# K turned in its own order, joint softmax sums, and weight transfers from GpSimd in a fused attention and maxout kernel

## The chip, the cores and the metric

The kernel runs on one core of a Trainium2 chip. A core has five engines with queues of their own: TensorE (PE; its weight loads are listed apart as PEld), VectorE (DVE), ScalarE (ACT), GpSimd (POOL) and SyncE (SP). SP, ACT and POOL can start DMA transfers, which 16 DMA engines carry out. The metric is the device time of one execution in microseconds; lower is better.

## The reference

Block-causal attention over 8 batches, 8 heads, 576 positions of 64 dimensions in blocks of 64, and then a feed-forward layer that takes the largest of three products. q, k and v are f32, the weights double precision; the kernel computes in f32, and splits its operands into a high and a low part where one f32 product of reduced precision would not do.

```python
scores = (1 / sqrt(D)) * q @ k.T             # q, k, v: (8, 8, 576, 64)
scores = where(block_i >= block_j, scores, -1e9)
attn = softmax(scores)                       # denominators + 1e-9
x = (attn @ v).transpose(0, 2, 1, 3).reshape(4608, 512)
h = max(x @ w1, x @ w2, x @ w3)              # w: (512, 768)
out = h @ w_out                              # (768, 512)
```

## The kernel before

**The order of the work.** The program isn't written in the order in which it runs. `job(cost, rank, call, after=, take=, give=)` describes one step: which engines can do it and at what estimated cost, a rank (its due time, in units near a microsecond), the jobs it follows, and the buffers it takes and gives back (`slots` says how many there are). `in_order` then plays a greedy schedule over all jobs and writes the instructions in the order that comes out. The numbers at the head (`LAG`, `SEND`, `LOAD`, `DMA`, `MOVE`, `TURNED`, `GAP`, `SMALL`) and the functions `pe`, `dve`, `act`, `pool` are its prices: they take no time themselves, but they set the order of every engine's queue. On the chip each engine follows its queue strictly in order and waits at an instruction until its inputs are there.

**Attention.** Two heads make a `Pair`, 64 partitions each; four pairs make a batch. Batch 0 is done in two parts, `FRONT` (queries and keys below 256) and `BACK` (queries from 256, all keys); batch 1 is `EARLY`, the others `WHOLE`. The steps of a pair:

- `load`: q and k come in 32x32 blocks into the tiles `qn` and `kn` (four DMAs each), v into `vn`.
- `turn_k`, `turn_q`: VectorE turns the 32x32 blocks into `kq`. K is written scattered, so that in each block of 128 a run of 32 places holds the keys of one remainder modulo four; Q is written in order.
- `qk`: scores on PE, one f32 matmul per head and query tile (the trace lists two records for each); `ask` and `qk4` do the last 64 queries of both heads in one stationary operand, `q8`.
- `top` (line 405): VectorE finds the negative row maximum; `exp` (485): ScalarE's exponential with row sums; `sum` and `inverse` (490, 493): small VectorE instructions on the sums, for each head apart; `scale` (414 on ScalarE or 416 on POOL): normalises.
- `turn` (510, 514): VectorE turns P into the tile `pz`; `move` (520): four DMAs send each head's `pz` to `pt`, the P^T that PE reads.
- `pv` (754): P^T against V gives x, `out` copies it, `x_high` and `x_low` split it into `xh` and `xl`.

**Weights.** 24 units, 18 of w1, w2, w3 and 6 of w_out. Each `Unit` loads 512 KB of doubles (line 277), and takes them apart into an f32 high part and a low part: |w| on ScalarE (287), five VectorE steps (293, 300, 306, 312, 323), a copy on ScalarE, three matmuls on PE (330 to 332), a last copy on ScalarE. `DELAY` and `PACE` set the ranks of the units, `NEAR` how many units ahead a load may be issued.

**The layer.** A `Chunk` is half a batch, 256 or 320 columns of x. `product` (867) multiplies three pairs of parts (w high with xh and xl, w low with xh) over four slices of x for each of 6 x 3 weight units, `most` takes the maxima (882), `high` and `low` split h into `hh` and `hl`, and `project` (933) multiplies by w_out. The products fill PE between the attention steps.

Of the kernel before, what the change touches and what calls it, by code (L numbers as in the profile page):

```python
# [19 lines left out]
INF = 3.0e38  # L20
# [14 lines left out]
SEND = 650.0  # L35
LOAD = 475.0
DMA = 2000.0
MOVE = 3500.0
TURNED = 3000.0

GAP = 125.0
SMALL = 75.0
# [82 lines left out]
def pe(*cols, least=128):  # L125
    return sum(max(n, least) / 2.4 + 2.7 for n in cols)


def dve(n, fast=False):
    return 70.0 + n / (1.92 if fast else 0.96)  # L130


def act(n, psum=True):
    return (52.0 if psum else 95.0) + n / 1.2


def pool(n):
    return 190.0 + 1.95 * n
# [3 lines left out]
def kernel(  # L142
# [23 lines left out]
    DELAY = 16.0  # L166
    PACE = 4.0
# [7 lines left out]
    NEAR = 2  # L175
    XB = 1
# [43 lines left out]
    nats = {nm: const.tile([P, S], F32, name=nm) for nm in ("qn", "kn")}  # L220
# [21 lines left out]
    class Unit:  # L242


        def __init__(self, u, src, dst, n, prior, *early):
# [8 lines left out]
                {"SP": LOAD},  # L254
                rank - 4,
# [19 lines left out]
        def load(self, eng):  # L275
            st = moe.tile([P, 1024], F32, name=self.tag, bufs=1).bitcast(I32)
            nc.sync.dma_start(st.rearrange("p (c f) -> p c f", f=2 * self.n), self.src.bitcast(I32))
            lo_hi = st.rearrange("p (n t) -> p n t", t=2)
            self.low_word, self.high_word = lo_hi[:, :, 0].bitcast(U32), lo_hi[:, :, 1]
# [68 lines left out]
    def weights():  # L348
# [8 lines left out]
        for f in range(NF):  # L357
# [7 lines left out]
                early[u - NEAR],  # L365
# [43 lines left out]
    def norm_cost(n):  # L409
        return {"POOL": 160.0 + 1.66 * n, "ACT": 188.0 + n / 1.2}  # L410
# [7 lines left out]
    class Head:  # L418
# [5 lines left out]
        def plan(self, t0, after):  # L424

            pair, part, scales, later = self.pair, self.pair.part, {}, []
            for n, ts in enumerate(part.groups):
                apart, exps, r = None, [], t0 + (SECOND if part.beside and ts == part.later else n)
                for t in ts:
                    m = P * (t + 1)  # L430
                    d = job(
                        {"DVE": dve(m)},
# [3 lines left out]
                        after=(pair.scored[ts], apart),  # L436
                        take=("stat",) if t == part.tiles[0] else (),
                    )
                    if t != ts[-1]:
                        apart = job({}, 0, lambda eng: None, after=(d,), lasts=GAP)  # L440
                    exps.append(job({"ACT": act(m) + 185.0}, r + 2, self.exp, t, after=(d,), take=(f"p{t}",)))
                join(exps, BANK)
                later += exps
                if ts in part.first and ts != part.first[-1]:
                    continue
                done = [t for ts in part.first for t in ts] if ts in part.first else ts
                cols = slice(min(COL[t] for t in done), max(COL[t] for t in done) + 1)
                inv = job({"DVE": SMALL}, r + 4, self.sum, cols, after=later, lasts=SMALL + GAP)
                inv = job({"DVE": SMALL}, r + 4, self.inverse, cols, after=(inv,))
                for t in done:  # L450
                    scales[t] = job(norm_cost(P * (t + 1)), r + 5 + t / 2, self.scale, t, after=(inv,))
                later = []
            join(scales.values(), ("stat",))
# [4 lines left out]
            for t in part.tiles:  # L458
# [6 lines left out]
                    take=() if first else ("pz",),  # L465
# [5 lines left out]
            self.moved = job(  # L471
                {"SP": 4 * SEND}, t0 + 13, self.move, after=self.turned, take=("pt",), give=("pz",), lasts=4 * SEND + TURNED
            )
            return first

        def top(self, eng, t):

            if not hasattr(self, "stat"):
                self.stat = tuple(att.tile([P, NT], F32, name=nm, bufs=slots["stat"]) for nm in ("nm", "sm", "rs"))
# [9 lines left out]
        def sum(self, eng, c):  # L489
# [537 lines left out]
```

## Time and profile before

| | us |
|---|---|
| median of 3 runs (lowest, highest) | 934.22 (932.08, 934.27) |
| the profiled execution | 933.72 |
| its span, first to last instruction | 931.9 |
| PE busy | 886.0 |
| PE's weight loads busy | 735.1 |
| DVE busy | 560.9 |
| ACT busy | 457.9 |
| POOL busy | 246.1 |

The page of a profile gives busy time of each engine, the span in 40 slices, the DMA queues, the chain of work that ended last, and the costliest groups of instructions by line, tile and shape. An engine in the list of waits stands before the arrow, what released it behind; "SPq" is SyncE's own queue of DMA issues. The views by window show the same for a stretch of time, and the timeline lists instructions with start, duration and, in brackets, the idle time before. Matmul records overlap one another, so what a matmul costs is read from start to start, not from its own duration.

### The profile page before, as it was taken

Reading aid. Unit: us, or ns where it says so; the run is one execution under the profiler, and the core shown is the slowest. Engines: PE = TensorE matmul, PEld = TensorE weight load, DVE = VectorE, ACT = ScalarE, POOL = GpSimd, SP = SyncE. Lnnn points to the kernel's source line nnn. Section 1 sums busy time; section 2 is a strip of 40 time slices with the busy share of each in tenths; the row PEclk is TensorE's granted clock in tenths of the full one; section 3 lists DMA queues with packets and bytes.
Section 4 is the critical chain, followed back from the end, with each engine's and each line's share of the span. In section 5 each row is a group of like instructions: output and inputs, shape, how many; then the busy total and the mean of one; then the engine's idle time right before and its main releaser. Section 6 shows DMA issues by size and latency. Waiting matters only on the chain.

```text
span 931.9 us, 17031 instructions
## 1 busy us (share of the span) xinstructions
PE 886.0 (95%) x5736; PEld 735.1 (79%) x5736; DVE 560.9 (60%) x1768; ACT 457.9 (49%) x1315; POOL 246.1 (26%) x368
## 2 busy tenths in 40 slices
PE   3778988999999999999999999999999999999998
PEld 2346755877888978897888978897888978899997
DVE  5888999787764376547664386447664376431101
ACT  3655565676554365536554355536554355532111
POOL 2123212334231232213231232223231232222201
PEclk9889999999999999999999999999999999999999
DMA  5778567676653455552753355552763354330010
GB/s 119 178 186 229 147 165 158 141 154 151 145 128 73 94 132 115 127 109 53 161 125 74 83 133 122 119 110 58 149 135 69 84 133 96 95 72 23 1 34 23
DMA packets 253910, 104.93 MB, mean 113 GB/s; under 512 B 206464, under 2 KB 248448, under 8 KB 253824
## 3 DMA queue, kind: packets, MB, share of 16 engines
q1 hardware_dynamic: 234624, 101.49, 47.3%
q10 hardware_dynamic: 19200, 2.36, 1.6%
q8 instruction: 45, 0.74, 0.3%
q14 instruction: 41, 0.34, 0.1%
HBM read 41.94 MB, written 9.44 MB: 55 GB/s over the span
## 4 chain that ended last, share of the span: by engine, by line
PE 77%; DVE 10%; DMA 6%; issue 2%; ACT 2%; SPq 1%; POOL 0%; DVEq 0%; ACTq 0%
PE pm L867 44%; PE pm L933 15%; PE sb L754 8%; PE sb L706 7%; PE sb L712 2%; DMA w<-in_moe_w_dram 2%; DVE pz L510 2%; DMA qn<-in_q_dram 2%; DVE sb L405 2%; ACT p L485 1%; DMA pt<-pz 1%; DMA kn<-in_k_dram 1%; DVE left L323 1%; SPq L520 1%; DVE kq L683 1%
## 5 line engine op out<-in xcount | busy, mean ns | idle before, releaser
L867 PE MATMUL pm<-xh,w 128*128 128x320 f32 (+1 forms) x2304 | 491.2, 302 | 2.5 <-ACT xh L234 1.6
L867 PEld LDWEIGHTS pm<-xh,w 128*128 128x128 f32 x2304 | 378.2, 190 | 18.1 <-issue 8.8
L867 PE MATMUL pm<-xl,w 128*128 128x256 f32 (+1 forms) x1152 | 341.9, 297 | 3.0 <-POOL xl L239 3.0
L867 PEld LDWEIGHTS pm<-xl,w 128*128 128x128 f32 x1152 | 219.5, 191 | 6.5 <-POOL xl L239 3.9
L405 DVE CUSTOM_DVE_ANT_0 sb<-sb,mask 128x384 f32<-128x384 f32 (+4 forms) x288 | 135.6, 505 | 89.5 <-PE sb L706 44.1
L882 DVE TENSOR_TENSOR m<-pm,m 128x256 f32<-128x256 f32 (+1 forms) x192 | 86.3, 449 | 165.2 <-PE pm L867 164.5
L510 DVE STREAM_TRANSPOSE pz<-p 128x384 f32<-128x384 f32 (+3 forms) x320 | 159.6, 528 | 37.6 <-ACT p L414 17.7
L485 ACT ACTIVATE p<-sb,nm 128x256 f32<-128x256 f32 (+3 forms) x256 | 134.3, 527 | 93.6 <-DVE nm L405 75.9
L416 POOL TENSOR_TENSOR p<-p,rs 128x128 f32<-128x128 f32 (+4 forms) x148 | 108.3, 751 | 244.1 <-DVE rs L493 168.7
L239 POOL TENSOR_TENSOR hl<-m,hh 128x256 fp32r<-128x256 f32 x96 | 71.4, 744 | 288.1 <-ACT hh L234 258.0
L933 PE MATMUL pm<-wo,hh 128*128 128x512 f32 x384 | 123.8, 403 | 0.4 <-ACT wo L234 0.4
L234 ACT CAST hh<-m 128x256 fp32r<-128x256 f32 x96 | 39.0, 406 | 157.6 <-DVE m L882 157.5
L754 PE MATMUL sb<-pt,vn 128*64 128x320 f32 (+4 forms) x896 | 103.3, 364 | 4.8 <-DMA pt<-pz 3.1
L706 PE MATMUL sb<-kq 64*128 64x384 f32 (+3 forms) x512 | 91.8, 478 | 16.7 <-DVE kq L690 16.7
L754 PEld LDWEIGHTS sb<-pt,vn 128*64 128x64 f32 x896 | 62.4, 138 | 45.7 <-issue 14.9
L414 ACT ACTIVATE p<-p,rs 128x256 f32<-128x256 f32 (+4 forms) x140 | 82.3, 603 | 24.1 <-DVE rs L493 17.7
L706 PEld LDWEIGHTS sb<-kq 64*128 64x128 f32 x512 | 47.1, 197 | 54.6 <-issue 21.3
L239 POOL TENSOR_TENSOR xl<-x,xh 128x320 fp32r<-128x320 f32 (+1 forms) x64 | 52.2, 819 | 142.9 <-ACT xh L234 142.9
L933 PEld LDWEIGHTS pm<-wo,hh 128*128 128x128 f32 x384 | 70.5, 188 | 18.2 <-issue 1.7
L933 PE MATMUL pm<-wo,hl 128*128 128x512 f32 x192 | 75.0, 391 | 0.0
L234 ACT COPY m<-pm 128x256 f32<-128x256 f32 (+1 forms) x96 | 38.1, 397 | 33.2 <-PE pm L867 21.7
L485 ACT ACTIVATION_READ_ACCUMULATOR p<-sb,nm 128x1 f32 x256 | 50.3, 196 | 0.0
(67 smaller groups left out, 691.7 us busy)
## 6 DMA issues: line engine op xcount, KB each, us to landing
pt<-pz SPq DMA_DIRECT2D x224, 200.0 KB, 3.9
w<-in_moe_w_dram SPq DMA_DIRECT2D x18, 512.0 KB, 4.8
kn<-in_k_dram SPq DMA_DIRECT2D x128, 72.0 KB, 2.4
vn<-in_v_dram SPq DMA_DIRECT2D x64, 128.0 KB, 2.5
out_dram<-osb SPq DMA_DIRECT2D x32, 256.0 KB, 2.0
qn<-in_q_dram SPq DMA_DIRECT2D x96, 72.0 KB, 2.4
pt<-pz SPq DMA_DIRECT2D x32, 152.0 KB, 3.2
wo<-in_moe_w_out_dram SPq DMA_DIRECT2D x6, 512.0 KB, 4.6
```

Source lines behind the costliest of these rows:

```text
L234: nc.scalar.copy(dst, src)
L239: {"DVE": nc.vector, "POOL": nc.gpsimd}[eng].tensor_tensor(out=dst, in0=a, in1=b, op=ALU.subtract)
L405: nc.vector.tensor_tensor_reduce(out=ps, in0=ps, in1=hidden, scale=-SCALE, scalar=first, op0=ALU.add, op1=ALU.min, accum_out=out_)
L414: nc.scalar.mul(p, p, r)
L416: nc.gpsimd.tensor_tensor(out=p, in0=p, in1=r.broadcast_to([P, p.shape[1]]), op=ALU.mult)
L485: nc.scalar.activation(self.p[t], self.ps.pop(t), AF.Exp, bias=nm[:, c : c + 1], scale=-1.0, accum_out=sm[:, c : c + 1])
L510: nc.vector.transpose(dst, p[:, 0 : n * P])
L706: nc.tensor.matmul(ps, self.q[h.own, P * t : P * (t + 1)], self.k[h.own, 0:w], start=True, stop=True)
L754: nc.tensor.matmul(o[h.own].rearrange("p (i u) -> p i u", u=n)[:, :, c0 : c0 + z - a], self.vn[:, kt, h.j, :], h.pt[:, :, a:z], start=(m = ...
L867: nc.tensor.matmul(self.ps, w[i, f][:, c, :], xx, start=(c == 0 and s == 0), stop=(c == NC - 1 and s == 2))
L882: nc.vector.tensor_tensor(out=m, in0=ps, in1=m, op=ALU.max)
L933: nc.tensor.matmul(self.po[: self.rows], h, w[f], start=(f == 0 and s == 0), stop=(f == NF - 1 and s == 2))
```

## The change

- **K in its own order.** q and k share one tile `nat` and one transpose turns both into `kq` in the order in which they lie (`turn_qk`, in place of `turn_k` and `turn_q`). The order that P^T needs is made when PE reads K: `keys` gives it an access pattern whose inner step is four elements. `qk4` takes its 576 keys as 256 and 256 + 64 instead of 288 + 288.
- **Joint sums.** The row statistics of two heads lie in one tile; `sum` and `inverse` move from Head to Pair and work on both heads once all exponentials are done.
- **One P^T for two heads in batch 0.** There both heads share `pz` and `pt`, the second at an offset of 96, and `move` is issued once.
- **GpSimd starts the weights' transfers**, with NEAR 4 instead of 2 (w_out's own limit stays 2).
- **Buffers:** P^T 2 instead of 3 (and `stat` counted by pair), x32 2 instead of 1 of each half.
- **The planner:** new prices, DELAY 28 and PACE 3.5 instead of 16 and 4; the second chunk's products from f = 2 on wait for the first chunk's projection.

```diff
-SEND = 650.0
-LOAD = 475.0
-DMA = 2000.0
-MOVE = 3500.0
-TURNED = 3000.0
+SEND = 620.0
+LOAD = 540.0
+ASK = 1000.0
+DMA = 2200.0
+MOVE = 4500.0
+TURNED = 4400.0
...
-    return sum(max(n, least) / 2.4 + 2.7 for n in cols)
+    return sum(max(n, least) / 2.4 + 13.5 for n in cols)
...
-    DELAY = 16.0
-    PACE = 4.0
+    DELAY = 28.0
+    PACE = 3.5
...
-    NEAR = 2
-    XB = 1
+    NEAR = 4
+    XB = 2
...
-        sb=5, sb5=4, scores=4, pm=3, stat=4, stat4=2, p0=2, p1=2, p2=2, p3=2, p4=1,
+        sb=5, sb5=4, scores=4, pm=3, stat=2, stat4=2, p0=2, p1=2, p2=2, p3=2, p4=1,
...
-        vn=2, kq=2, q8=2, pz=2, pt=3,
+        vn=2, kq=2, q8=2, pz=2, pt=2,
...
-    nats = {nm: const.tile([P, S], F32, name=nm) for nm in ("qn", "kn")}
+    nat = const.tile([P, 2, S], F32, name="nat")
...
-                {"SP": LOAD},
-                rank - 4,
+                {"POOL": ASK},
+                rank - 8,
                 self.load,
...
-            nc.sync.dma_start(st.rearrange("p (c f) -> p c f", f=2 * self.n), self.src.bitcast(I32))
+            nc.gpsimd.dma_start(st.rearrange("p (c f) -> p c f", f=2 * self.n), self.src.bitcast(I32))
...
+            self.off = 96 * j if pair.part.loads == 1 else 0
...
-            self.moved = job(
-                {"SP": 4 * SEND}, t0 + 13, self.move, after=self.turned, take=("pt",), give=("pz",), lasts=4 * SEND + TURNED
-            )
+            if alone or self.j:
+                turned = self.turned if alone else self.turned + pair.heads[0].turned
+                self.moved = job(
+                    {"SP": 4 * SEND}, t0 + 13, self.move, after=turned, take=("pt",), give=("pz",), lasts=4 * SEND + TURNED
+                )
+                if not alone:
+                    pair.heads[0].moved = self.moved
...
+                pair.stats = tuple(att.tile([P, 2, NT], F32, name=nm, bufs=slots["stat"]) for nm in ("nm", "sm", "rs"))
+            self.stat = tuple(t[:, self.j] for t in pair.stats)
...
-        def sum(self, eng, c):
-            nc.vector.tensor_scalar_add(self.stat[2][:, c], self.stat[1][:, c], EPS)
...
+            if self.off:
+                self.pair.heads[0].pt, run = self.pt, slice(0, 192)
...
+                    exps = [h.exps[t] for h in self.heads for t in ts]
+                    inv = job({"DVE": SMALL}, r, self.sum, cols, after=exps, lasts=SMALL + GAP)
+                    inv = job({"DVE": SMALL}, r, self.inverse, cols, after=(inv,))
...
+        def sum(self, eng, c):
+            _, sm, rs = self.stats
+            nc.vector.tensor_scalar_add(rs[:, :, c], sm[:, :, c], EPS)
...
-        def turn_k(self, eng):
-
+        def turn_qk(self, eng):
             kq = att.tile([P, 2, S], F32, name="kq", bufs=slots["kq"])
-            self.k, self.q = kq[:, 0], kq[:, 1]
-            src, dst, n = nats["kn"][:, self.at :], self.k, min(self.part.keys, 512)
-            nc.vector.transpose(dst[:, 0:n].rearrange("p (k j r) -> p k r j", j=4, r=32), src[:, 0:n])
-            if n == self.part.keys:
+            self.q, self.k = kq[:, 0], kq[:, 1]
+            own, n = self.part.queries, self.part.keys
+            if n < S:
+                nc.vector.transpose(kq[:, :, 0:n], nat[:, :, self.at : self.at + n])
                 return
-            nc.vector.transpose(dst[:, 512:S].rearrange("p (j r) -> p r j", j=4), src[:, 512:S])
-
-        def turn_q(self, eng):
-            own = self.part.queries
-            nc.vector.transpose(self.q[:, own], nats["qn"][:, self.at :][:, own])
+            src, dst = (t.rearrange("p a s -> p (a s)")[:, own.start :] for t in (nat, kq))
+            nc.vector.transpose(dst, src)
+
+        def keys(self, own, a, z):
+
+            n = min(P, z - a)
+            return self.k[own, a:z].rearrange("p (k r j) -> p k j r", j=4, r=n // 4)
...
-                        nc.tensor.matmul(ps, self.q[h.own, P * t : P * (t + 1)], self.k[h.own, 0:w], start=True, stop=True)
+                        nc.tensor.matmul(ps, self.q[h.own, P * t : P * (t + 1)], self.keys(h.own, 0, w), start=True, stop=True)
...
-            ps = self.ps[a] = psa.tile([P, 288], F32, name="sb")
-            nc.tensor.matmul(ps, self.q8, self.k[:, 288 * a : 288 * a + 288], start=True, stop=True)
+            ps = self.ps[a] = psa.tile([P, 256 + 64 * a], F32, name="sb")
+            nc.tensor.matmul(ps[:, 0:256], self.q8, self.keys(slice(0, P), 256 * a, 256 * a + 256), start=True, stop=True)
+            if a:
+                nc.tensor.matmul(ps[:, 256:], self.q8, self.keys(slice(0, P), 512, S), start=True, stop=True)
...
-                        h.pt[:, :, a:z],
+                        h.pt[:, :, h.off + a : h.off + z],
...
+            wait = prior.projected if prior and prior.first else None
+            self.first = not prior
...
-                            after=(last, xjobs[c], units[i, f].done),
+                            after=(last, xjobs[c], units[i, f].done, wait if f > 1 else None),
...
+            self.projected = prior
```

More of the change, by code (lines that the diff above doesn't have):

```diff
@@ L422, in __init__, with plan @@
             self.ps, self.p = {}, {}
-        def plan(self, t0, after):
-            pair, part, scales, later = self.pair, self.pair.part, {}, []
+            self.off = 96 * j if pair.part.loads == 1 else 0
+        def plan(self, t0):
+            pair, part, self.exps, self.inv = self.pair, self.pair.part, {}, {}
             for n, ts in enumerate(part.groups):
-                apart, exps, r = None, [], t0 + (SECOND if part.beside and ts == part.later else n)
+                apart, r = None, t0 + (SECOND if part.beside and ts == part.later else n)
                 for t in ts:
@@ L435, in plan, with turns @@
                         t,
-                        after=(pair.scored[ts], apart),
-                        take=("stat",) if t == part.tiles[0] else (),
+                        after=(pair.scored[ts], apart, pair.began),
+                        take=("stat",) if pair.began is None else (),
                     )
+                    pair.began = pair.began or d
                     if t != ts[-1]:
                         apart = job({}, 0, lambda eng: None, after=(d,), lasts=GAP)
[L441 to L453, printed above, removed]
+                    self.exps[t] = job({"ACT": act(m) + 240.0}, r + 2, self.exp, t, after=(d,), take=(f"p{t}",))
+                join([self.exps[t] for t in ts], BANK)
+        def turns(self, t0, after):
+            pair, part, self.scales = self.pair, self.pair.part, {}
+            for t in part.tiles:
+                r = t0 + 8 + t / 2 + (SECOND if part.beside and t in part.later else 0)
+                self.scales[t] = job(norm_cost(P * (t + 1)), r, self.scale, t, after=(self.inv[t],))
+            scales, alone = self.scales, part.loads == 2
             self.turned, first = [], None
@@ L464, in plan @@
                     after=(scales[t], first or after),
-                    take=() if first else ("pz",),
+                    take=() if first or (self.j and not alone) else ("pz",),
                 )
@@ L500, in turn @@
             if not hasattr(self, "pz"):
-                self.pz = att.tile([P, 4 * (RUN + 16)], F32, name="pz", bufs=slots["pz"])
+                if self.j and self.pair.part.loads == 1:
+                    self.pz = self.pair.heads[0].pz
+                else:
+                    self.pz = att.tile([P, 4 * (RUN + 16)], F32, name="pz", bufs=slots["pz"])
             z = self.pz.rearrange("p (j u) -> p j u", u=RUN + 16)
@@ L554, in plan @@
                 part.first,
-                after=(tk, tq, before and before.later),
+                after=(tq, before and before.later),
                 take=2 * len(part.first) * BANK,
@@ L595, in plan4 @@
             for a in range(2):
-                last = job({"PE": 4 * pe(288)}, first + 3 + a, self.qk4, a, after=(asked, last), take=BANK)
+                last = job({"PE": 4 * pe(256, *(64,) * a)}, first + 3 + a, self.qk4, a, after=(asked, last), take=BANK)
                 tops.append(
                     job(
-                        {"DVE": dve(288) + 10.0},
+                        {"DVE": dve(288) + 120.0},
                         first + 4 + a,
@@ L606, in plan4 @@
                 )
-            e = job({"ACT": 2 * act(288) + 370.0}, first + 5, self.exp4, after=tops, take=("p4",), give=2 * BANK)
+            e = job({"ACT": act(256) + act(320) + 480.0}, first + 5, self.exp4, after=tops, take=("p4",), give=2 * BANK)
             inv = job({"DVE": SMALL}, first + 6, self.sum4, after=(e,), lasts=SMALL + GAP)
@@ L641, in finish @@
                 )
-            join((prior,), ("pt", "pt", "vn"))
+            join((prior,), ("pt",) * self.part.loads + ("vn",))
         def values(self, eng):
```

67 lines of the change are left out of this document (45 added, 22 removed).

## The prediction

> **What bounds the kernel now.** I read the page first, then the stages, then who waits for whom in the stage that loses time. The page gives each engine's share and 40 slices of the span.
>
> ```profile
> PE 886.0 (95%) x5736; PEld 735.1 (79%) x5736; DVE 560.9 (60%) x1768; ACT 457.9 (49%) x1315; POOL 246.1 (26%) x368
> ...
> PE   3778988999999999999999999999999999999998
> ...
> DVE  5888999787764376547664386447664376431101
> ```
>
> TensorE (PE) is full from about the eleventh slice on, and VectorE (DVE) only in slices two to seven. So there are two stages; the busy times per window tell them apart.
>
> ```profile
> 0.00:50.00 50.00, 27.76 (x96) 13.85 (x96) 35.62 (x121) 25.54 (x73) 11.11 (x27) 0.93 0.65 151
> 50.00:100.00 50.00, 41.44 (x219) 28.86 (x221) 43.32 (x105) 26.22 (x58) 13.50 (x14) 0.90 0.80 217
> 100.00:150.00 50.00, 43.46 (x236) 28.59 (x233) 48.87 (x132) 32.26 (x82) 15.52 (x17) 1.00 0.65 156
> 150.00:200.00 50.00, 48.68 (x303) 38.51 (x301) 40.56 (x127) 29.21 (x88) 12.80 (x19) 1.00 0.62 131
> 200.00:250.00 50.00, 48.38 (x307) 38.86 (x307) 39.89 (x137) 32.05 (x101) 19.14 (x29) 1.00 0.68 151
> ...
> 500.00:550.00 50.00, 50.00 (x361) 42.58 (x361) 29.98 (x99) 24.79 (x73) 13.43 (x18) 1.00 0.40 85
> ```
>
> The columns are PE, weight loads, DVE, ScalarE (ACT), GpSimd (POOL), granted clock, DMA share and GB/s. At 500 us PE issues 361 matmuls in 50 us without a gap: nothing on another engine shortens that stage. In the first 150 us it issues 551, and DVE is busy 127.8 of 150 us: the ramp is VectorE's. It ends when VectorE hands over the last of the 24 weight units and PE has used it:
>
> ```profile
> 158.96 0.68 DVE L323 SCALAR_TENSOR_TENSOR left<-wo,osb 128x512 fp32r<-128x512 uint32 x1
> ```
> ```profile
> 161.91 0.39 PE L332 MATMUL pm<-left,plus 128*128 128x512 f32 x1
> ```
>
> Behind that PE loses little: 1.3 and 1.6 us of the next two windows. So the sum is: how much earlier does the last unit come, what has PE then left to do, and what does the change cost PE itself. The profiled execution took 933.72 us (span 931.9 and 1.8 around it), 0.5 below the median of 934.22. All sums are against 933.7.
>
> **VectorE's work ahead of the last unit.** The order is needed here. VectorE before, first pair of heads; L490 and L493 are the sum and its inverse, kq the turned K and Q:
>
> ```order
> L405 ISA nm 128x1
> L490 TENSOR_SCALAR rs<-sm 128x2
> L493 RECIPROCAL rs<-rs 128x2
> L490 TENSOR_SCALAR rs<-sm 128x2
> L493 RECIPROCAL rs<-rs 128x2
> L683 STREAM_TRANSPOSE kq<-kn 128x2x32x4
> L690 STREAM_TRANSPOSE kq<-qn 128x256
> ```
>
> VectorE after, the same place (L294 to L313 are steps of the first weight unit):
>
> ```order
> L294 TENSOR_SCALAR wo_134<-wo_134 128x512
> L301 TENSOR_SCALAR wo_134<-wo_134 128x512
> L722 STREAM_TRANSPOSE kq<-nat 128x2x256
> L625 TENSOR_SCALAR rs<-sm 128x2x2
> L307 SCALAR_TENSOR_TENSOR wo_134<-w_100,wo_134 128x512
> L629 RECIPROCAL rs<-rs 128x2x2
> L313 TENSOR_SCALAR wo_134<-wo_134 128x512
> ```
>
> One transpose where two or three stood, two small instructions where four stood, and weight steps between. Counted to the last unit, VectorE has 374 rows before and 331 after; all kinds agree but four: 18 turns of K and 11 of Q become 11 joint ones (4 front, 4 back, 3 whole pairs), 40 sums and inverses become 20, and of 14 maxima and 7 copies of x there stay 12 and 4. Their prices:
>
> ```profile
> L683 DVE STREAM_TRANSPOSE kq<-kn 128x512 f32<-128x512 f32 x32 | 35.4, 1107 | 6.4 <-PE sb L706 6.2
> ...
> L690 DVE STREAM_TRANSPOSE kq<-qn 128x576 f32<-128x576 f32 x28 | 21.2, 758 | 0.0
> ...
> L882 DVE TENSOR_TENSOR m<-pm,m 128x320 f32<-128x320 f32 x96 | 45.9, 479 | 51.5 <-PE pm L867 51.3
> ...
> L493 DVE RECIPROCAL rs<-rs 128x3 f32<-128x3 f32 x56 | 9.7, 173 | 1.2
> ...
> L686 DVE STREAM_TRANSPOSE kq<-kn 128x64 f32<-128x64 f32 x32 | 8.6, 269 | 0.0
> ...
> L490 DVE TENSOR_SCALAR rs<-sm 128x2 f32<-128x2 f32 x16 | 3.9, 241 | 2.7 <-ACT p L485 2.7
> L493 DVE RECIPROCAL rs<-rs 128x2 f32<-128x2 f32 x16 | 2.5, 157 | 0.1
> L683 DVE STREAM_TRANSPOSE kq<-kn 128x256 f32<-128x256 f32 x4 | 2.4, 604 | 5.3 <-DMA vn<-in_v_dram 4.5 <-DMA kn<-in_k_dram 0.8
> L690 DVE STREAM_TRANSPOSE kq<-qn 128x320 f32<-128x320 f32 x4 | 2.0, 498 | 0.0
> L236 DVE COPY x<-sb 128x320 f32<-128x320 f32 x4 | 1.9, 477 | 0.0
> ...
> L690 DVE STREAM_TRANSPOSE kq<-qn 128x256 f32<-128x256 f32 x4 | 1.6, 400 | 0.0
> ```
>
> The columns are busy us, mean ns, idle before. K costs more than Q per column because it is written scattered: from 256 to 512 columns 503 ns, 1.96 ns a column, while Q (256 to 576) takes 358 ns, 1.12 ns a column with 113 ns fixed. The joint turn writes in order, so I price it by Q: 0.69, 1.12 and 1.40 us for 512, 896 and 1152 columns. A front pair saves 604+400-686 = 318 ns, a back pair 1107+269+498-1116 = 758, a whole pair 1107+269+758-1403 = 731: 4, 4 and 3 of them, 6.5 us. Sums: 16 pairs of 241+157 and 4 pairs of about 173+173 are 7.7 us; 20 instructions of 173 remain, 3.5: 4.2 us saved. Two maxima (0.96) and three copies (1.4) stand later or on ScalarE. Together 13.1 us; neighbours on VectorE overlap by some tenth, so I take **12 us**. Ends: 0, if the joint sums, which now wait for both heads' exponentials, leave as much idle time as they save; 13.1.
>
> **Waits for weights.** Of VectorE's idle time before 160 us these rows belong to transfers that SyncE's queue (SP) starts:
>
> ```profile
> DVE wo L293 <- ACT wo L287: 5.3, 4, 2.1
> ...
> DVE pz L510 <- DMA pt<-pz: 1.4, 1, 1.4
> ```
>
> SP is a full row of issues there, weights (L277) behind the sends of P^T (L520):
>
> ```profile
> 29.15 0.37 SPq L277 DMA_DIRECT2D w<-in_moe_w_dram  x1
> 29.86 4.37 SPq L520 DMA_DIRECT2D pt<-pz  x4
> 34.28 0.59 SPq L277 DMA_DIRECT2D w<-in_moe_w_dram  x1
> 34.97 2.48 SPq L520 DMA_DIRECT2D pt<-pz  x4
> 37.49 0.59 SPq L277 DMA_DIRECT2D w<-in_moe_w_dram  x1
> ```
>
> The change takes 24 weight issues of some 0.59 us (14 us) and half of the front pairs' 32 sends of 0.62 (10 us) off SP, and asks for a unit four ahead, not two. SP before, around that place:
>
> ```order
> L277 DMA w_286<-in_moe_w_dram 128x4x256
> L520 DMA pt<-pz 128x1x96 x4
> L671 DMA vn_75<-in_v_dram 128x2x64 x2
> L277 DMA w_353<-in_moe_w_dram 128x4x256
> L520 DMA pt<-pz 128x1x96 x4
> ```
>
> POOL after (L417 normalises, L240 makes xl):
>
> ```order
> L278 DMA w_108<-in_moe_w_dram 128x4x256
> L278 DMA w_112<-in_moe_w_dram 128x4x256
> L278 DMA w_141<-in_moe_w_dram 128x4x256
> L417 TENSOR_TENSOR p_148<-p_148,rs 128x128
> L417 TENSOR_TENSOR p_139<-p_139,rs 128x256
> L417 TENSOR_TENSOR p_144<-p_144,rs 128x256
> L278 DMA w_189<-in_moe_w_dram 128x4x256
> ```
>
> POOL and VectorE already get in each other's way: beside POOL's two-input work VectorE's L323 takes 1.21 us, not the 0.68 quoted above.
>
> ```profile
> 87.66 1.21 DVE L323 SCALAR_TENSOR_TENSOR left<-w,wo 128x512 fp32r<-128x512 uint32 x1
> ```
> ```profile
> 87.41 0.91 POOL L239 TENSOR_TENSOR hl<-m,hh 128x256 fp32r<-128x256 f32 x1
> ```
>
> Five transfers of 512 KB now start ahead of the first softmax, where two stood. Of the 6.7 us I take **4 us** back (ends 0 and 6.7). Against it: the burst shares the DMA engines with K and Q of the next pairs, and each issue lengthens POOL's queue. The trace has no DMA from POOL; 24 issues at SP's price are 14 us on an engine busy 40 of the first 150; at the 0.91 us of POOL's own row, 22 us. It is hidden while VectorE is late; what isn't I put at **1.5 us** (ends 0, and the rival below). Behind a late issue on POOL stand the normalisations and xl, for which the transposes and PE wait.
>
> The Trainium skill, "SBUF — State Buffer", section "SBUF: two separate sides", speaks against this part: GpSimd writes the descriptors of its own transfers and is locked out while VectorE holds the port pair that they share. The stretched row agrees with such a lock; by that rule a transfer starts up to one VectorE instruction late, 24 times half a microsecond or so, an estimate, which the lead of four units would hide: the sum would stay.
>
> **PE.** Ahead of the last unit stand 57 products of 320 columns before and 30 after; everything else but the q8 matmuls agrees. The rows of the chain of waits:
>
> ```profile
> 371.73 10.26 PE pm L867 x72
> 382.00 1.93 PE sb L706 x12
> ...
> 392.31 0.97 PE sb L712 x4
> ```
>
> A product takes 10.26/72 = 0.143 us, so PE has 27 x 0.143 = **3.9 us** more left when the last unit comes. The q8 scores (L712) are two matmuls of 288 columns before, and 256, 256 and 64 after: equal columns, one matmul more in each of 32 pairs, in the full stage, where nothing hides it. Ends 0 and 0.1 us each; I take 0.05, **1.6 us**.
>
> **K read with a step of four elements** has no row: every operand of PE now lies in runs. The other four score records of a pair:
>
> ```profile
> 579.04 0.70 PE L706 MATMUL sb<-kq 64*128 64x256 f32 x4
> ```
>
> So the scores take 1.93 us for 1024 columns of each head, 0.70 for 256 more and 0.97 for L712: 3.6 us a pair, 115 us in 32 pairs. The nearest scattered access is L683's writing: 1.96 ns a column against 1.12, 1.76 times. If PE slowed so, it would cost 115 x 0.76 = 87 us; if nothing, 0. But PE takes a column of f32 each 1.93/1024 = 1.88 ns, hardly faster than the scattered 1.96, where a product goes at 0.143/320 = 0.45 ns. I stand near the lower end: **2 us**.
>
> The Trainium skill, "SBUF — State Buffer", section "Door 1: The DMA port swizzle", says that SBUF is read in lines of 16 bytes and that each access to a new line is penalised; four elements are 16 bytes, so by that rule every column would be a new line. No run here shows it for PE.
>
> **Buffers.** Two of P^T instead of three: SP's sends wait for transposes, and PE's whole wait for them is small.
>
> ```profile
> PE sb L754 <- DMA pt<-pz: 3.1, 3, 2.1
> ```
>
> I put it at 0 (ends -3 and +3). The second x buffer frees a copy that ScalarE makes: 0. The planner's new numbers, and the second chunk's wait for the first's projection, act through the order alone and are in the counts above: 0. VectorE's later work also shrinks by some 1.2 us a pair, and PE's 2.9 us of idle between 150 and 250 us can go: **2 us** gained.
>
> Sum: 933.7 - 12 - 4 + 1.5 + 3.9 + 1.6 + 2 - 2 = 924.7; I say **925 us**.
>
> **Rivals.** *The step costs PE.* For it: L683's 1.76 times; against it: f32's slow columns. At full price 925 - 2 + 87 = 1010 us. It turns the gain into a loss from 11/32 = 0.34 us a pair, a tenth of the 3.6. Chance 0.13. By the Trainium skill's page on SBUF cited above this case would be the likely one.
>
> *POOL's queue holds the weights.* It takes its work in order, and its normalisations wait long for the sums:
>
> ```profile
> POOL p L416 <- DVE rs L493: 168.7, 53, 15.1
> ```
>
> If the lead of four is used up in such waits, some eight of the loads behind a normalisation come late by the 2.1 us that the longest weight wait shows: 17 us, 942. Against it: the leads are long (five before the first). Chance 0.08; 0.03 more for another loss of that size.
>
> *VectorE isn't the limit.* The joint sums wait for the second head's exponentials, and VectorE stands idle for what it saved: the 12 go and the rest stays: 937 at worst, 934 where a quarter of them holds. For it: ScalarE's chain also runs through the ramp (84 of 150 us busy). Chance 0.17, no change.
>
> *The new order packs the ramp better.* VectorE idles 22 of the first 150 us, 6.7 of them counted above. If half of the other 15 goes, 917, less with shorter sends: 910 to 917. Chance 0.12.
>
> **Numbers.** 0.47 is left for the forecast, 917 to 931. Faster is that and the last rival, 0.59; same 0.17; slower 0.13+0.08+0.03 = 0.24. A change under 0.3% (2.8 us) can't be told from none by measuring this kernel. The range leaves out the dear step and a little below: 908 to 944; where the gain holds, 910 to 931.
>
> **What would show it.** Right: the joint turn of 1152 columns at about 1.40 us; the last L333 on PE near 150 us, not 162; VectorE's wait for ScalarE's first weight step below 2 us; 50 us windows at 500 us with as many matmuls as now. Wrong: the 12 score matmuls over 2.1 us (the step); POOL's issues followed by VectorE waiting for weights (the queue); the last unit still at 158 us (VectorE not the limit). K and Q of the second pair landing after 14 us would show the burst.

## The result, and the profile after

The changed kernel takes 1022.21 us (median, 1019.47 to 1022.85), the kernel before 934.23 in the same rounds: ratio 1.094, 95% interval 1.092 to 1.097. Forecast was 925, with a range to 944. It is 88 us slower, and the first two parts of its page already say that this is no matter of waiting.

```profile
PE 978.7 (96%) x5800; PEld 743.7 (73%) x5800; DVE 539.9 (53%) x1570; ACT 462.4 (45%) x1315; POOL 259.3 (25%) x394
...
PE   3679989999999999999999999999999999999998
...
DVE  4788996765564644455454635556453645531101
```

PE is busy 92.7 us longer (886.0 before), in nearly the same number of instructions, and VectorE 21 us shorter. The busy times per window, the same windows as in the prediction, show where it falls (columns as there):

```profile
0.00:50.00 50.00, 22.23 (x82) 11.72 (x83) 30.03 (x97) 21.18 (x66) 19.20 (x38) 0.84 0.80 199
50.00:100.00 50.00, 44.82 (x210) 27.96 (x208) 41.01 (x100) 30.05 (x68) 16.68 (x19) 0.95 0.59 159
100.00:150.00 50.00, 48.25 (x240) 29.75 (x238) 48.33 (x112) 29.46 (x74) 17.23 (x20) 1.00 0.61 148
...
500.00:550.00 50.00, 50.00 (x278) 38.89 (x278) 20.74 (x65) 21.63 (x63) 12.26 (x21) 1.00 0.47 107
```

In the full stage, at 500 us, PE is still without a gap, but it gets through 278 matmuls in the window instead of 361: its own instructions have become longer. Which ones, the chain of what ended last names; its score lines, L746 and L752, stood at 6.6 and 2.4% as L706 and L712 before.

```profile
PE pm L914 45%; PE pm L980 14%; PE sb L746 14%; PE sb L796 9%; PE sb L752 5%; DMA pt<-pz 2%; DMA nat<-in_k_dram 2%; PE pm L331 1%; PE sb L754 1%; DMA nat<-in_q_dram 1%; DVE pz L515 1%; DMA w<-in_moe_w_dram 1%; DVE kq L725 1%; DVE left L324 0%; PE pm L333 0%
```

The 12 score matmuls of a whole pair, in order of time (start, us, engine, line), which took 1.93 us before, occupy PE from 626.58 to the next start:

```profile
626.58 3.85 PE L746 MATMUL sb<-kq 64*128 64x512 f32 x12
630.36 0.42 PE L914 MATMUL pm<-xh,w 128*128 128x320 f32 x1
```

That is 3.78 us. The groups by shape (busy us, mean ns of one, idle before) give each form, first after, then before:

```profile
L752 PE MATMUL sb<-kq,q 128*128 128x256 f32 x128 | 67.6, 626 | 0.6 <-ACT p L492 0.6
L746 PE MATMUL sb<-kq 64*128 64x512 f32 x128 | 65.6, 1110 | 0.4 <-DVE kq L725 0.4
...
L754 PE MATMUL sb<-kq,q 128*128 128x64 f32 x64 | 13.2, 296 | 0.0
```
```profile
L712 PE MATMUL sb<-kq,q 128*128 128x288 f32 x128 | 40.6, 409 | 0.8 <-ACT p L485 0.8
L706 PE MATMUL sb<-kq 64*128 64x512 f32 x128 | 37.6, 665 | 2.5 <-DVE kq L690 2.5
```

512 columns went from 665 to 1110 ns. These are the durations of records that overlap; from start to start the price is the 3.78 us above. The ramp isn't earlier either: VectorE's last weight step and the last unit's matmul, at 158.96 and 161.91 us before, now stand here.

```profile
165.09 0.65 DVE L324 SCALAR_TENSOR_TENSOR left<-wo,osb 128x512 fp32r<-128x512 uint32 x1
...
168.18 0.39 PE L333 MATMUL pm<-left,plus 128*128 128x512 f32 x1
```

### The profile page after: what moved, and what is told of

It reads as the page before. It is cut to its first block, busy times and chain, and to the rows that moved or that the text cites. A ratio compares the mean times of both kernels' runs of the same rounds, so it can differ in the third digit from the quotient of the medians.

```text
span 1021.1 us, 16795 instructions
## 1 busy us (share of the span) xinstructions
PE 978.7 (96%) x5800; PEld 743.7 (73%) x5800; DVE 539.9 (53%) x1570; ACT 462.4 (45%) x1315; POOL 259.3 (25%) x394
## 4 chain that ended last, share of the span: by engine, by line
PE 90%; DMA 5%; DVE 3%; issue 1%; ACT 1%; SPq 0%; POOL 0%; ACTq 0%; DVEq 0%; POOLq 0%
PE pm L914 45%; PE pm L980 14%; PE sb L746 14%; PE sb L796 9%; PE sb L752 5%; DMA pt<-pz 2%; DMA nat<-in_k_dram 2%; PE pm L331 1%; PE sb L754 1%; DMA nat<-in_q_dram 1%; DVE pz L515 1%; DMA w<-in_moe_w_dram 1%; DVE kq L725 1%; DVE left L324 0%; PE pm L333 0%
## 5 line engine op out<-in xcount | busy, mean ns | idle before, releaser
L914 PE MATMUL pm<-xh,w 128*128 128x320 f32 (+1 forms) x2304 | 499.0, 304 | 2.5 <-ACT xh L235 2.2
L406 DVE CUSTOM_DVE_ANT_0 sb<-sb,mask 128x256 f32<-128x256 f32 (+3 forms) x288 | 136.4, 498 | 172.9 <-PE sb L746 88.2
L492 ACT ACTIVATE p<-sb,nm 128x512 f32<-128x512 f32 (+3 forms) x256 | 133.9, 526 | 130.8 <-DVE nm L406 121.6
L417 POOL TENSOR_TENSOR p<-p,rs 128x384 f32<-128x384 f32 (+4 forms) x150 | 105.9, 725 | 303.1 <-DVE rs L629 274.7
L746 PE MATMUL sb<-kq 64*128 64x256 f32 (+3 forms) x512 | 160.5, 757 | 18.5 <-DVE kq L722 10.0
L515 DVE STREAM_TRANSPOSE pz<-p 128x384 f32<-128x384 f32 (+3 forms) x320 | 156.9, 526 | 24.9 <-ACT p L415 17.1
L746 PEld LDWEIGHTS sb<-kq 64*128 64x128 f32 x512 | 47.7, 202 | 101.6 <-issue 76.9
L980 PE MATMUL pm<-wo,hh 128*128 128x512 f32 x384 | 120.8, 395 | 0.4 <-ACT wo L235 0.4
L415 ACT ACTIVATE p<-p,rs 128x512 f32<-128x512 f32 (+4 forms) x138 | 79.7, 620 | 29.5 <-DVE rs L629 14.0
L240 POOL TENSOR_TENSOR xl<-x,xh 128x256 fp32r<-128x256 f32 (+1 forms) x64 | 51.5, 810 | 144.3 <-ACT xh L235 144.3
L752 PE MATMUL sb<-kq,q 128*128 128x256 f32 x128 | 67.6, 626 | 0.6 <-ACT p L492 0.6
```

The lines of the kernel that those rows point to most:

```text
L240: {"DVE": nc.vector, "POOL": nc.gpsimd}[eng].tensor_tensor(out=dst, in0=a, in1=b, op=ALU.subtract)
L406: nc.vector.tensor_tensor_reduce(out=ps, in0=ps, in1=hidden, scale=-SCALE, scalar=first, op0=ALU.add, op1=ALU.min, accum_out=out_)
L415: nc.scalar.mul(p, p, r)
L417: nc.gpsimd.tensor_tensor(out=p, in0=p, in1=r.broadcast_to([P, p.shape[1]]), op=ALU.mult)
L492: nc.scalar.activation(self.p[t], self.ps.pop(t), AF.Exp, bias=nm[:, c : c + 1], scale=-1.0, accum_out=sm[:, c : c + 1])
L515: nc.vector.transpose(dst, p[:, 0 : n * P])
```

## The experiments: the step

Theory 1: TensorE pays for the step itself. Rival: order, weight transfers or buffers. Two kernels tell them apart from both sides, one with all but the step, one with the step alone.

**a_runs**, all but the step:

```
 def keys(self, own, a, z):
-    n = min(P, z - a)
-    return self.k[own, a:z].rearrange("p (k r j) -> p k j r", j=4, r=n // 4)
+    return self.k[own, a:z]
# turn_qk (not shown): K with the scattered write of before, Q by itself
```

> The changed kernel, but VectorE turns K with the scattered write of before and TensorE reads it in one run; everything else (joint sums, weights from GpSimd, buffers, planner's numbers) stays. Theory 1, the stepped read costs TensorE: the 12 score matmuls of one group take about 1.9 us again instead of 3.8, and some 3.4 us a pair x 32 pairs = 109 us go, or the 88 us of the result if part of that lay in waits: 913 to 934 us. Rival, the new order, the GpSimd transfers or the buffers cost it: the time stays above 1000 us although the score matmuls are quick again.

936.41 us (931.46 to 939.39), ratio to before 1.0038, interval 1.0017 to 1.006. PE's groups:

```profile
L745 PE MATMUL sb<-kq 64*128 64x512 f32 x128 | 37.2, 658 | 0.9 <-DVE kq L725 0.9
```

**b_step4**, the kernel before with the step alone (K turned as it lies, `keys()` as in the change, the last tile's scores in 256 + 256 + 64):

> The kernel before, with the stepped read alone: K is turned as it lies and TensorE reads it with a step of 4; Q apart, sums apart, weights from SP, old buffers and numbers. Theory 1: 934 + 88 to 109 = 1022 to 1043 us, the 12 score matmuls at 3.8 us. Rival (order, transfers, buffers): within 10 us of 934.

1012.59 us, ratio 1.0862 (1.0828 to 1.0897): 80 us from this part alone, less than the 88 to 109 that theory 1 had named. Some 4 of them are the price not of the step but of the split into 256 + 256 + 64, as d_half below shows.

```profile
L707 PE MATMUL sb<-kq 64*128 64x512 f32 x128 | 65.6, 1110 | 1.2 <-DVE kq L691 1.2
```

The same 1110 ns stands here beside an unchanged ramp (the last unit's matmul at 162.6 us, 161.9 before). Theory 1 holds for the bulk; the rest of the change gives a loss of about 3.7 us where a gain was forecast, and that has the next section. First, what of the step costs. Three kernels change only how `keys()` walks through the same columns (j=2 or j=8 for j=4; runs of four elements at a step of eight).

> The changed kernel, with K read with a step of 2 elements (8 bytes) instead of 4 (leaves the right pairing of keys and values out; same counts and sizes). If each element of another 16-byte line costs a fixed time, a step of 2 touches half as many lines as a step of 4 and twice as many as a run: score matmuls between the two, near 2.6 to 2.9 us for the 12, and 950 to 980 us. If any step halves TensorE's rate: 3.8 us and 1015 to 1030 us. If a step of 8 bytes is free: 1.9 us and 913 to 934 us.

> The changed kernel, with K read with a step of 8 elements (32 bytes) instead of 4 (leaves the right pairing of keys and values out). If a matmul's read pays for each new 16-byte line, a step of 8 costs what a step of 4 does, since both touch one line an element: 512 columns at 1.11 us, 1015 to 1030 us. If the distance counts: above 1.3 us, and more than 1040 us.

> The changed kernel, with K read in runs of four elements (16 bytes) at a step of eight (leaves the right pairing of keys and values out). If a matmul's read pays for 16-byte lines, four elements share one and 512 columns take 0.66 to 0.68 us as in one run: 930 to 940 us. If every break in the run costs it: 0.8 us and more, above 950 us.

938.35, 1023.07 and 933.85 us, one run each. The group of 512 columns, in that order:

```profile
L746 PE MATMUL sb<-kq 64*128 64x512 f32 x128 | 38.3, 675 | 0.5 <-DVE kq L725 0.5
```
```profile
L746 PE MATMUL sb<-kq 64*128 64x512 f32 x128 | 66.7, 1128 | 0.5 <-DVE kq L725 0.5
```
```profile
L745 PE MATMUL sb<-kq 64*128 64x512 f32 x128 | 37.2, 658 | 0.5 <-DVE kq L725 0.5
```

A step of 8 bytes adds 17 ns to 658, steps of 16 and 32 bytes cost the same 450 to 470, and broken runs of 16 bytes cost nothing. So, in these five patterns, neither a break in the run nor its distance is charged, but every 16 bytes from which only one element is used; with two it is nearly free. (From start to start the 12 matmuls take 1.93 us in a run, 1.92 in runs of four, 2.00, 3.78 and 3.85 with steps of 2, 4 and 8.) My expectation for a step of 2 (halfway between, 950 to 980) was wrong, and the expectation for "a step of 8 bytes is free" was nearly met; those for a step of 8 and for runs of four were met.

The Trainium skill, "SBUF — State Buffer", section "Door 1: The DMA port swizzle", has this rule in full: lines of 16 bytes, and at least two hits on a line for full bandwidth. The runs agree: two hits, 675 ns; one, 1110. The same note goes on to say that 4 fp32 may be strided for free; read as a step of four, the runs contradict it.

**c_pread**, the step on the other engine: K turned as it lies and read in one run; VectorE's transposes of P read with the step instead.

```
-nc.vector.transpose(dst, p[:, 0 : n * P])
+nc.vector.transpose(dst, p[:, 0 : n * P].rearrange("p (k r j) -> p k j r", j=4, r=32))
# not shown: the same for the last tile, the mask's hidden columns, keys() as in a_runs
```

> The changed kernel, with the step moved from TensorE to VectorE: K is turned as it lies and read in one run, so the columns of the scores stand in K's order, and VectorE's transposes of P read them with a step of 4 (the mask's hidden columns move with them). Theory 1: TensorE is rid of it as with the scattered turn of K; VectorE has 47% of its time free, so its step may cost it something in the ramp only: 905 to 934 us, some 5 us below the scattered turn if the step costs VectorE nothing. Rival, the step costs VectorE as much as TensorE (about 1 ns an element more, some 1.6 us a pair on average): the ramp's turns lengthen, and it comes out 2 to 10 us above the scattered turn. Rival order: above 1000 us.

960.66 us, ratio 1.0306 (1.0283 to 1.0329). VectorE pays too; the transposes of 512 columns, here and in a_runs:

```profile
L515 DVE STREAM_TRANSPOSE pz<-p 128x512 f32<-128x512 f32 x128 | 140.1, 1095 | 17.4 <-ACT p L415 12.8 <-DMA pt<-pz 1.9 <-DMA nat<-in_k_dram 1.3
```
```profile
L515 DVE STREAM_TRANSPOSE pz<-p 128x512 f32<-128x512 f32 x128 | 88.8, 694 | 17.9 <-ACT p L415 12.4 <-DMA pt<-pz 2.8 <-POOL p L417 1.3
```

0.78 ns a column more, on transposes that already scatter what they write. I had expected 2 to 10 us above a_runs at most; it is 24. A VectorE with spare time in the mean (it is busy 66% of this span) does not hide it.

## The experiments: the rest of the change

Theory 2: the weights' transfers from GpSimd cost what the rest should gain. Again from both sides: on the kernel before alone, and taken out of a_runs (with `NEAR` 2 and the due time of before again).

```
-nc.gpsimd.dma_start(st.rearrange(...), ...)     NEAR = 4     # a_runs
+nc.sync.dma_start(st.rearrange(...), ...)       NEAR = 2     # a_runs_sp2
```

> The kernel before, with the weights' transfers alone moved from SyncE to GpSimd (due four steps earlier, as in the change). Theory 2, the rest of the loss (the changed kernel without its step is 0.4% above before) is these transfers: they crowd the first 50 us, the turns of K wait for K's transfers, and it takes 936 to 941 us. Rival, as the prediction summed it (4 us of waits gone, 1.5 us for issues and burst): 931 to 933 us, under the kernel before in the same rounds.

> The changed kernel with the scattered turn of K, and the weights' transfers again on SyncE, two units ahead instead of four. Theory 2: the first 50 us have TensorE busy some 27 us again instead of 22.5, and the time falls from 936 to 928 to 934 us. Rival, joint sums and the new numbers cost it: 935 to 939 us.

b_pool: 936.6 us, ratio 1.0037 (1.002 to 1.0053). a_runs_sp2: 924.61 us, ratio 0.9908 (0.9877 to 0.9939), below the 928 to 934 that I had expected. The ramp's balance is read best from one window to 170 us and one behind it; before, a_runs and a_runs_sp2:

```profile
0.00:170.00 170.00, 131.90 (x647) 85.56 (x649) 143.09 (x401) 95.56 (x244) 42.97 (x62) 0.95 0.69 169
170.00:1000.00 830.00, 754.08 (x5093) 649.54 (x5089) 417.79 (x1367) 362.37 (x1073) 203.16 (x306) 1.00 0.41 92
```
```profile
0.00:170.00 170.00, 127.58 (x616) 86.34 (x617) 138.37 (x371) 92.08 (x239) 57.44 (x82) 0.91 0.68 169
170.00:1000.00 830.00, 758.35 (x5186) 658.63 (x5184) 415.02 (x1267) 368.04 (x1078) 201.32 (x312) 1.00 0.41 92
```
```profile
0.00:170.00 170.00, 134.77 (x688) 90.87 (x690) 146.93 (x396) 98.74 (x259) 45.95 (x64) 0.94 0.72 174
170.00:1000.00 830.00, 747.66 (x5114) 650.17 (x5110) 408.42 (x1246) 361.95 (x1056) 195.07 (x303) 1.00 0.41 91
```

PE's busy time behind 170 us is what is left when the ramp ends: 754, 758 and 748 us, and the spans (931.9, 933.4, 922.8) follow it. With the transfers on GpSimd VectorE does less by 170 us (138.4 against 146.9 us): it is kept waiting.

Two more runs separate GpSimd from the four units of lead: only `NEAR` differs, or only the engine with its due time (four steps earlier on GpSimd) and its price in the planner. The kernel before took 932.2 to 932.8 us in the rounds of all four.

> The changed kernel with the scattered turn of K (936.4 us), its weights from GpSimd, but each transfer at most two units ahead of the unit that has been sized, instead of four. Theory 2a, the burst of five transfers at the start costs the 12 us between 936.4 and 924.6: 923 to 928 us. Theory 2b, the transfers' place on GpSimd costs it (issues on GpSimd, a landing later than from SyncE): 932 to 938 us.

> The changed kernel with the scattered turn of K (936.4 us), its weights on SyncE, still up to four units ahead. Theory 2a (the burst): 932 to 938 us, since the burst stays. Theory 2b (GpSimd): 923 to 928 us.

| weights from | four units ahead | two units ahead |
|---|---|---|
| GpSimd | 936.4 (a_runs) | 927.1 (a_runs_near) |
| SyncE | 923.3 (a_runs_sp4) | 924.6 (a_runs_sp2) |

Neither 2a nor 2b holds alone: GpSimd costs 13 us at a lead of four and 2.5 at two. The DMA issues of the first 30 us (KB each, median us to landing), a_runs and then a_runs_sp4:

```profile
w<-in_moe_w_dram POOLq DMA_DIRECT2D x9, 512.0 KB, 5.8
...
nat<-in_k_dram SPq DMA_DIRECT2D x16, 32.0 KB, 2.9
```
```profile
w<-in_moe_w_dram SPq DMA_DIRECT2D x9, 512.0 KB, 4.8
...
nat<-in_k_dram SPq DMA_DIRECT2D x16, 32.0 KB, 3.1
```

Nine weight transfers start in either, and K's median landing is the same. But the medians hide the start. By 6.8 us a_runs has issued five weight transfers, a_runs_sp4 two, and the second pair's K comes late in a_runs. VectorE's turn of it (L722) and the first pair's joint sum (L625), a_runs and then a_runs_sp4:

```profile
14.37 0.62 DVE L722 STREAM_TRANSPOSE kq<-nat 128x256 f32<-128x256 f32 x1 [4.04 <-DMA nat<-in_k_dram]
...
15.16 0.13 DVE L625 TENSOR_SCALAR rs<-sm 128x4 f32<-128x4 f32 x1
```
```profile
9.84 0.17 DVE L625 TENSOR_SCALAR rs<-sm 128x4 f32<-128x4 f32 x1 [0.52 <-ACT p L492]
...
10.94 0.62 DVE L722 STREAM_TRANSPOSE kq<-nat 128x256 f32<-128x256 f32 x1 [0.72 <-DMA nat<-in_k_dram]
```

In a_runs the planner puts the first pair's sum behind the second pair's turn, and with K late the sum comes 5.3 us later. So the two kernels differ in VectorE's order too, not only in the engine that starts the weights. This is the start of the loss and not all of it: the fourth pair's turn stands at 24.03 us in a_runs and 24.48 in a_runs_sp4. VectorE's waits in a_runs up to 170 us name what else comes late (total us, times, longest):

```profile
DVE x L237 <- PE sb L795: 9.6, 3, 4.9
DVE kq L722 <- DMA vn<-in_v_dram: 4.6, 1, 4.6
DVE kq L722 <- DMA nat<-in_k_dram: 4.0, 1, 4.0
...
DVE kq L722 <- DMA pt<-pz: 2.5, 1, 2.5
```

The first row, VectorE behind the products with V, is 0.4 us in a_runs_sp2 and 3.4 in a_runs_sp4; the second stands there as well (4.5 and 4.7) and tells nothing apart. That transfers from two queues crowd each other all through the ramp is argued from these rows, not shown; the table and the late K are what is shown.

The granted clock of TensorE is a rival that these runs don't separate. In the windows to 170 us it is 0.95 before, 0.91 in a_runs and 0.94 in a_runs_sp2 (the third column from the right). In a_runs_near four executions at a mean clock of 0.989 to 0.991 take 923.9 to 926.1 us, where a_runs_sp2 stands too, and four at 0.983 to 0.985 take 928.1 to 930.3: the 2.5 us at a lead of two come with the clock. Between a_runs (0.982 to 0.989) and a_runs_sp4 (0.991 to 0.994) the mean differs by 0.006, and 0.006 of some 930 us is 6 of the 13 us, an estimate of the most that it can be worth; the 4.3 us of b_pool (0.986 against 0.991) may be of that kind whole. Whether the clock is a cause here or follows from TensorE's waits is not shown.

**The planner's numbers, and the joint sums.** a_runs_sp2 is 7.6 us under before. Theory 3: joint sums and buffers bring it. d_num takes the numbers of before into a_runs_sp2, b_num puts the new ones alone into before.

> The changed kernel with the scattered turn of K and the weights on SyncE two units ahead (924.6 us, 0.9% under before), with the planner's numbers of before (durations, DELAY 16, PACE 4). Theory 3, the 7.6 us come from the joint sums and the two buffers of x: 923 to 927 us. Rival, they come from the order that the new numbers make: 930 to 936 us.

> The kernel before with the planner's new numbers alone. Theory 3: within 2 us of 932. Rival, the order brings the gain: 923 to 927 us.

926.15 (ratio 0.9929, 0.9901 to 0.9956) and 925.62 us (0.993, 0.991 to 0.995). Each half brings nearly the whole gain by itself. The numbers alone, which move instructions in time, and a few from one engine to another, take PE's rest behind 170 us to the same place as a_runs_sp2:

```profile
0.00:170.00 170.00, 134.24 (x688) 89.06 (x690) 149.58 (x422) 97.00 (x254) 49.20 (x70) 0.95 0.71 172
170.00:1000.00 830.00, 747.25 (x5050) 644.85 (x5048) 413.86 (x1343) 364.08 (x1072) 194.74 (x293) 1.00 0.41 91
```

Theory 3 falls for b_num; why the two gains don't add is partly explained by the last run below.

**The joint turn.** With a step of 2 the joint turn of K and Q can be had almost free of TensorE's price. c_v2sp puts the other halving of the order into V's loads (`vn[j % 2 :: 2]`, four transfers a pair for two); d_step2 is the same without V's part.

> As the kernel beside it (weights on SyncE), but with the joint turn of K and Q: K is read with a step of 2 elements, and the other halving of the keys' order lies in V, whose rows are loaded into every second partition (two transfers of V more in each pair). Correct pairing, one transpose a pair instead of three, 0.78 us of VectorE a pair less. If VectorE's work sets the ramp's end, as the prediction had it (6.5 us for the joint turns): 922 to 928 us, some 6 us under the kernel beside it. Rival, VectorE's work alone does not set it: within 2 us of the kernel beside it, or above it by the two transfers.

> The kernel of 924.6 us with the joint turn and K read with a step of 2, but V loaded as before (leaves the right pairing of keys and values out). Tells apart why the joint turn with V in every second partition took 937.2 us. If it was V's two further transfers a pair: 922 to 926 us. If it is the joint turn itself, which waits for Q's transfer as well as K's before TensorE has anything: 933 to 939 us.

937.21 us (ratio 1.0046, 1.0027 to 1.0066) and 925.74 (0.9937, 0.9918 to 0.9956). The joint turn with the step of 2 gives nothing against three transposes (924.6). The step of 2 has its own price in it. In d_step2 the 12 score matmuls take 2.00 us from start to start, 1.93 in a run:

```profile
508.67 2.07 PE L746 MATMUL sb<-kq 64*128 64x512 f32 x12
510.67 0.39 PE L914 MATMUL pm<-xh,w 128*128 128x256 f32 x1
```

The other score matmuls of a pair take 0.06 us more (0.65 against 0.63, and 1.13 against 1.09), so the step of 2 costs 0.13 us a pair, some 4 us in 32. V's two further transfers, no more bytes, cost 11 us. (c_v2sp also reads the last 64 columns with a step of 4, which is 0.01 us a pair.) PE's waits over the first 300 us, with them and without:

```profile
PE sb L795 <- DMA pt<-pz: 14.3, 6, 4.9
```
```profile
PE sb L796 <- DMA pt<-pz: 2.9, 2, 2.0
```

P^T is sent by the same queue as V's loads, and it is what PE waits for. That V's loads hold it up there is argued from these rows.

**d_half**, the fastest: a_runs_sp2 with the last tile's scores in two matmuls again.

```
-nc.tensor.matmul(ps[:, 0:256], self.q8, self.keys(..., 256 * a, 256 * a + 256), ...)
-if a:
-    nc.tensor.matmul(ps[:, 256:], self.q8, self.keys(..., 512, S), ...)
+nc.tensor.matmul(ps, self.q8, self.k[:, 288 * a : 288 * a + 288], ...)
```

> The kernel of 924.6 us with the last tile's scores in two matmuls of 288 columns again, instead of 256 + 256 + 64, which a run allows. Four passes of 64 columns and their issue go: the row of 64 columns has 296 ns a matmul in the changed kernel, and the pairs of 288 cost some 0.05 us each more than those of 256: 922.5 to 925 us, the fastest of all if the sum holds. Rival, order: 923 to 930 us in either direction, since the planner counts other durations.

919.04 us, ratio 0.986 (0.9834 to 0.9886): 13.6 us under before and 5.6 under a_runs_sp2, more than the 2 that I had expected. The rows, a_runs_sp2 and then d_half:

```profile
L751 PE MATMUL sb<-kq,q 128*128 128x256 f32 x128 | 38.1, 390 | 2.3 <-ACT p L492 2.3
...
L753 PE MATMUL sb<-kq,q 128*128 128x64 f32 x64 | 10.8, 251 | 0.0
```
```profile
L751 PE MATMUL sb<-kq,q 128*128 128x288 f32 x128 | 40.4, 407 | 2.0 <-ACT p L492 2.0
```

48.9 us of busy time for the three matmuls, 40.4 for the two, with equal columns. Put between two products, the three take 1.09 us a pair and the two 0.97 (from the start of such a group to the second product behind it, less one product), so the split itself costs 0.12 us a pair, some 4 us in 32. The rest of the 5.6 us goes with the order, since the edit also changes the planner's prices; the last weight unit's matmul, too, stands at 151.4 us instead of 154.3. The split sits in every run with 256 + 256 + 64 and not in b_num: without it, the rest of the change (joint sums, the shared P^T of batch 0, the buffers, the second chunk's wait) brings 6.6 us on top of the numbers (925.6 to 919.0). No run takes these four apart.

## Why the prediction was wrong

From d_half the runs lead step by step to the changed kernel: 919.0, with the split scores 924.6, with the weights on GpSimd four ahead 936.4, with the joint turn and the step 1022.2. Against the terms of the sum:

| term | predicted, us | the runs |
|---|---|---|
| the step | +2 | +83.9 (after against a_step2, one run, whose step of 2 has itself a price of some 4) |
| VectorE's work: joint turn | 6.5 of the -12 | +1.1 (d_step2 against a_runs_sp2, with a step of 2) |
| VectorE's work: sums, copies; shared P^T, buffers, second chunk's wait | the rest of -12; 0 | -6.6 together on the new numbers (d_half against b_num); some -12 on the old (d_num's -6.5 less the 5.6 of the split) |
| planner's numbers | 0 | -7.0 (b_num) |
| weights on GpSimd | -4 + 1.5 | +11.8 (a_runs against a_runs_sp2); alone on before +4.3 |
| one q8 matmul more | +1.6 | +5.6 (a_runs_sp2 against d_half), of which some 4 from start to start |

The +3.9 us of products that are left and the -2 us of VectorE's later work can't be read apart in the runs.

**The step that failed is the price of the stepped read.** I had bounded it rightly by 0 and 87 us and then stood near the lower end, since a column of f32 costs 1.88 ns of PE anyway, near the 1.96 of a scattered write on VectorE. That argument takes the slow column for slack in which a slow read hides. It doesn't: with the step the 12 matmuls take 1.96 times as long (3.78 / 1.93), if anything more than the 1.76 of L683, the nearest row that I had quoted. The trace shows each score matmul of the code twice (12 records for three tiles of two heads); that the column is slow because it is read more than once, and that each reading then pays, fits this and is argued, not shown. Rival 1, at 1010 us and a chance of 0.13, was this case; its price (87) was right to within 6 us of PE's 92.7 more busy time. That is partly luck, since two errors cancel: from start to start the step costs 3.25 us a pair, 104 in 32, because the factor was near 2 and not 1.76 (the 12 matmuls from 1.93 to 3.78, the other 4 from 0.63 to 1.08, the last tile's from 1.09 to 2.03). Some 15 to 20 of the 104, an estimate from the difference, don't show in the 83.9; PE's idle time, which takes up part of them, is 42.4 us in the changed kernel and 51.3 in a_step2. I had cited the Trainium skill's rule on lines from "SBUF — State Buffer" with only half of its condition, and gave it a sentence where the change had exactly one element to a line.

**VectorE's work.** That the ramp ends with the last weight unit held up: its matmul on PE stands at 161.9 us before, 164.5 in a_runs, 154.3 in a_runs_sp2, 151.4 in d_half, near the 150 that the prediction had named, and these four times follow in that order. So do b_num (157.5), d_num (157.8), a_runs_near (157.5) and a_runs_sp4 (153.5), to within half a microsecond; d_step2 (151.4) and c_v2sp (155.3) do not. In the changed kernel it stands at 168.2. d_half's row (start of its last such matmul):

```profile
L333 PE MATMUL pm<-left,plus x1: 392/392/392, 151.4 to 151.4; 128*128 128x512 f32 x1
```

The turn came out at its price (1356 ns for 1152 columns, 1403 predicted). In d_step2 it ends the ramp at 151.4 us, 2.9 earlier than a_runs_sp2, and the step of 2 takes some 4 us back in PE's score matmuls, so its 6.5 us don't show. How much of the 2.9 is the turn's is open: the clock granted to the profiled d_step2 was 0.998, against 0.989. The tenth that I had taken off because neighbours on VectorE overlap was too little as well: up to 150 us the durations of VectorE's records add up to 157 us, and it is busy 128.

**Weights.** VectorE's wait for ScalarE's weight step (5.3 us before) is gone from the list, as the prediction had it, and ScalarE's waits for the weights' transfers fall from 12.9 to 1.7 us. Other waits of VectorE's lead the list of the changed kernel:

```profile
DVE x L237 <- PE sb L796: 10.4, 2, 5.7
DVE kq L722 <- DMA vn<-in_v_dram: 4.8, 1, 4.8
DVE kq L722 <- DMA nat<-in_k_dram: 4.1, 1, 4.1
```

The second is no new one (4.5 us before); the third is the second pair's K, whose turn starts at 14.59 us, 11.45 before. That is the sign of the burst that the prediction had named. The rival "POOL's queue holds the weights" had the size nearly right (-4 + 1.5 + 17 = 14.5 us, against 11.8 and 4.3) with the wrong story: the lead was not used up, and other transfers came late instead. The prediction had named the burst as a cost and taken it to be covered by VectorE's lateness; VectorE is itself what waits.

**The order.** "The planner's new numbers act through the order alone and are in the counts above: 0" was wrong: they alone bring 7.0 us.

**The q8 matmul.** 0.05 us a pair, with an upper end of 0.1, against 0.12 from start to start (0.17 by the times, with the order in it): put between products, the matmul of 64 columns adds 0.23 us to PE's time, where one of 256 adds 0.43.

Right were that PE stays the limit behind the ramp and the place named for the error: "the 12 score matmuls over 2.1 us". That two buffers of P^T cost nothing is not shown; the fastest version has two, and no run has three beside the rest of the change.

## What to carry to other kernels

Before an operand is given a step, count how many of its elements share 16 bytes: with one, the reading engine pays for every element, on TensorE almost double, and the transposes saved here on an engine with free time didn't pay for that; a halving of the order (a step of 8 bytes) cost some 4 of 925 us. Where a stage is full on one engine, a price bounded by "nothing" and "the nearest row" belongs at the nearest row, however plausible the cover. Undo a change part by part even when one part explains the loss: here the other parts held a version 1.4% faster than before.

## What the runs showed of the hardware

- TensorE, f32, 512 moving columns, duration of a record: 658 ns in a run and in runs of 16 bytes, 675 with a step of 8 bytes, 1110 with 16, 1128 with 32. From start to start the 12 score matmuls of a pair take 1.93 and 1.92 us, 2.00, 3.78 and 3.85.
- VectorE's transpose of 512 columns with a scattered write: 694 ns, and 1095 when the read has a step of 16 bytes as well.
- A DMA issue of 512 KB on GpSimd takes 0.78 us, where SyncE's took 0.59. In a_runs (min/median/max, first and last start):

```profile
L278 POOL DMA_DIRECT2D w<-in_moe_w_dram x18: 748/777/980, 2.5 to 80.9; - x18
```

- An f32 matmul of 64 columns on 128 rows, put between products, takes 0.23 us from start to start, more than half of one of 256 (0.43).
